# A routed-expert kernel whose token list gets rows of 16 equal words

## The chip, the cores and the metric

The kernel runs on one core of one Trainium2 chip. The metric is device time in microseconds of one execution, inputs and outputs in device memory. Five engines work side by side, each on its own instruction stream: TensorE (PE, with its weight loads PEld), VectorE (DVE), ScalarE (ACT), GpSimd (POOL) and SyncE (SP), which only issues transfers here. Transfers go through 16 DMA engines that all queues share; SP's plain transfers are queue q1 of the profile, POOL's indexed transfers are queue q0.

## The reference

```
# attention: a key counts for a query only if both fall to the same centroid
q_assign = argmax(q_n @ c_n, -1);  k_assign = argmax(k_n @ c_n, -1)
attn_out = softmax(where(q_assign == k_assign, q @ k.T / 8, -1e9)) @ v   # batch 2, 8 heads, 768 x 64
x = attn_out as (1536 tokens, 512)
# routed experts: one of 8 for each token
logits = x @ w_gate + modality_bias[modality_id];  e_idx = argmax(logits, 1)
for e in range(8):
    mask = e_idx == e
    out[mask] = gate_w[mask, None] * (relu(x[mask] @ w1[e]) @ w2[e])     # 512 -> 1024 -> 512
# a dense layer with softplus: 512 -> 2048 -> 512
return softplus(out @ w_in) @ w_out
```

## The kernel before, in words

**Attention.** The 16 pairs of batch and head are walked in 96 query tiles of 128 rows (6 a head). Tile g issues the score matmuls of tile g + 2, the transposes of tile g, and small jobs that a table hangs on g. The mask of a head pair is written into 16 partitions of the score operands `qB` and `kB` by four small SP transfers (`put_mask`, L295). After each head pair the attention rows go to `x_rows` in device memory (L394): each of 768 rows gets a run of 128 fp32 words, 512 bytes.

**Routing.** The tokens are routed in two batches of 768. `route_rank` gives each token a row number in `token_list`, a table in device memory: expert e owns rows from 1536 e on, with further rows for a late unit. The tokens of one expert stand one behind the other in their order. `scatter_list` (L594) then writes the token's number to that row: six indexed transfers on POOL, one for each 128 tokens, from column t of the tile `tokid`, through the helper `scatter` (L586), which also sets a spacer between two of them (L588, L589). The list starts out filled with the number 65536, which stands for "no token": `init_list` (a job of tile 7) sets up constants on POOL, fills the tile `empty` and stores it with one SP transfer (L1035, L1036).

**Expert units.** The expert stage is a written-out sequence of steps. A unit is a slice of one expert's list, of 256, 128 or 32 tokens. `u_list` (L754) reads the unit's token numbers with an SP transfer into the tile `it`, one word to a partition and column; `u_gather` (L768) clamps them on POOL into `gi` (L772) and fetches the 2 KB token rows with indexed transfers into `xg` (L776); `u_xpose` transposes `xg` on TensorE (L785); two layers follow (`l1_part` L818, `l2_part` L843), and the result rows go to `y_rows` with indexed transfers, 2 KB a row, again through `scatter`. Units 0 and 1 take tokens of the first batch alone; all later ones wait for the second batch's list. In the sequence, the transposes of unit 2 stand on TensorE ahead of the second layer of unit 1.

**Queues.** SP issues in program order, and so does POOL. On SP the first list read after the second `scatter_list` stands between weight loads (L730, L736): the loads written behind it are issued after it. Each weight chunk of 512 KB is split into two parts by ACT and by DVE or POOL (L740, L741) before TensorE uses it.

**The end.** When all units are written, `y_rows` is read back, and the dense layer runs over six blocks of 256 tokens (L1489, L1524).

Of the kernel before, what the change touches and what calls it, by code (L numbers as in the profile page):

```python
# [12 lines left out]
U32 = mybir.dt.uint32  # L13
# [19 lines left out]
def body(ctx, tc, qT, kT, vP, cen, mod, wg, bias, w1, w2, win, wout, out):  # L33
    nc = tc.nc
# [4 lines left out]
    NT = S // 128  # L39
# [2 lines left out]
    DUMMY = E * CAP  # L42
    LATE = DUMMY + 256 * NF
    LROWS = LATE + 256
    NM = N // 256
    CW = 1024
    pe, dve, act, pool, sp = nc.tensor, nc.vector, nc.scalar, nc.gpsimd, nc.sync

    xd = nc.dram_tensor("x_rows", (N, DM), F32, kind="Internal").ap()
    yd = nc.dram_tensor("y_rows", (N, DM), F32, kind="Internal").ap()  # L50
    lst = nc.dram_tensor("token_list", (LROWS, 1), U32, kind="Internal").ap()
    wf = nc.dram_tensor("w_rows", (16, 128, 1024), F32, kind="Internal").ap()

    const = ctx.enter_context(tc.tile_pool(name="const", bufs=1))
# [10 lines left out]
    def ctile(shape, dt, name):  # L65
        return const.tile(shape, dt, name=name)
# [2 lines left out]
    desc8 = ctile([128, E], F32, "desc8")  # L69
    tri = ctile([128, 128], BF16, "tri")  # L70
    ones = ctile([128, 128], BF16, "ones")
    tokid = ctile([128, 2 * NT], U32, "tokid")
    gate = ctile([128, 2 * NT], F32, "gate")
    lbias = ctile([128, 2 * NT, E], F32, "lbias")
    lacc = [ctile([128, NT, E], F32, f"lacc{b}") for b in range(2)]
# [29 lines left out]
    def setup_late():  # L105
        pool.iota(desc8, pattern=[[-1, E]], base=E, channel_multiplier=0, allow_small_or_imprecise_dtypes=True)
        pool.iota(e_off, pattern=[[CAP, E]], base=0, channel_multiplier=0, allow_small_or_imprecise_dtypes=True)
        pool.iota(tokid, pattern=[[128, 2 * NT]], base=0, channel_multiplier=1)
        pool.memset(e_row, 0.0)
        pool.iota(e_row[0:1], pattern=[[0, NT + 1], [CAP, E]], base=0, channel_multiplier=0, allow_small_or_imprecise_dtypes=True)  # L110
        pool.memset(e_row[0:1, NT, :], 0.0)
        pool.iota(iota_u, pattern=[[1, 16]], base=0, channel_multiplier=0, allow_small_or_imprecise_dtypes=True)
        pool.iota(u_fix, pattern=[[0, 3], [1, NK]], base=0, channel_multiplier=0, allow_small_or_imprecise_dtypes=True)
        for i, b in enumerate((128, 32, 0)):
            pool.iota(thr[:, i, :], pattern=[[256, 6]], base=b, channel_multiplier=0, allow_small_or_imprecise_dtypes=True)
        dve.tensor_reduce(out=fold, in_=ident.rearrange("p (g t) -> p t g", g=4), axis=AX.X, op=ALU.add)
        pool.iota(x_row, pattern=[[CAP, 9]], base=0, channel_multiplier=0, allow_small_or_imprecise_dtypes=True)
        pool.memset(ones, 1.0)
        pool.memset(tri, 1.0)
        pool.affine_select(  # L120
            out=tri, in_=tri, pattern=[[1, 128]], base=0, channel_multiplier=-1,
            compare_op=ALU.is_gt, fill=0.0,
        )
        pool.memset(pre9, 1.0)
        pool.affine_select(
            out=pre9, in_=pre9, pattern=[[1, 9], [-1, E]], base=0, channel_multiplier=0,
            compare_op=ALU.is_gt, fill=0.0,
        )
        pool.memset(drow, 0.0)
        pool.memset(nunit, 0.0)  # L130
        pool.memset(d_row, 0.0)
# [11 lines left out]
    p_1 = at.enter_context(tc.tile_pool(name="m1", bufs=1))  # L143
# [442 lines left out]
    def scatter(kind, **kw):  # L586

        pool.memset(spacer, 0.0)  # L588
        ins = pool.indirect_dma_start(**kw)  # L589
        for o in scattered[kind] + (scattered["y"] if kind == "late" else []):  # L590
            tc.declare_no_dep(ins.ins, o.ins, reason="rows are all different")
        scattered[kind].append(ins)

    def scatter_list(b, idx):  # L594
        for t in range(NT):
            scatter(
                "list", out=lst, out_offset=bass.IndirectOffsetOnAxis(ap=idx[:, t:t + 1], axis=0),
                in_=tokid[:, b * NT + t:b * NT + t + 1], in_offset=None,
            )

    def pick_early(cnt):
# [152 lines left out]
    def u_list(u, eng=sp):  # L754
        b = u["base"]
        if not isinstance(b, int):
            b = eng.value_load(b, min_val=0, max_val=DUMMY + 256 * (NF - 1))
        it = small.tile([128, 2], U32, tag="it", name="it", bufs=NF + NHU + NTU + 3)
        gi = small.tile([128, 2], U32, tag="gi", name="gi", bufs=NF + NHU + NTU + 3)
        with nc.allow_non_contiguous_dma(reason="token lists are columns of words"):  # L760
            if u["tiny"]:
                eng.dma_start(out=it[:32, 0:1], in_=lst[bass.ds(b, 32)])
            else:
                n = u["n"]
                eng.dma_start(out=it[:, :n], in_=lst[bass.ds(b, 128 * n)].rearrange("(j p) o -> p (j o)", p=128))
        u["it"], u["gi"] = it, gi

    def u_gather(u):  # L768
# [175 lines left out]
    with tc.manual_schedule():  # L944
# [57 lines left out]
        for p in range(1, 8):  # L1002
            b = 12 * (p - 1)
# [24 lines left out]
                    busy.add(g0 + k)  # L1028
            after.setdefault(g0 + 4, []).append((cv_store, (j,)))

        e_t = p_1.tile([128, LROWS // 128], U32, name="empty")

        def init_list():
            setup_late()
            pool.memset(e_t, int(EMPTY))  # L1035
            sp.dma_start(out=lst.rearrange("(p c) o -> p (c o)", p=128), in_=e_t)  # L1036
# [14 lines left out]
        def r0_scatter():  # L1051
            scatter_list(0, tmp["idx"])
            for i, u in enumerate((U0, U1)):
                u["eap"] = early[0:1, 2 * i:2 * i + 1]
                u["base"] = early[0:1, 2 * i + 1:2 * i + 2]
# [4 lines left out]
        job(65, route_carry)  # L1060
        job(80, route_gate, 0)
        job(81, lambda: u_list(U0))
        job(82, lambda: u_list(U1))
        job(84, lambda: u_gather(U0))
        ch0 = {}
# [26 lines left out]
        for g in range(NH * NT):  # L1092
            h, t = divmod(g, NT)
# [66 lines left out]
        for i in range(NEARLY, LF + 1):  # L1160
            t = i - NEARLY
# [144 lines left out]
        for k in loads[1]:  # L1306
            load(k)
        splits(1)
        scatter_list(1, idx)
        for f in range(4):  # L1310
            l1_part(U0, 1, f)
# [20 lines left out]
        def y_T(u, j):  # L1332
            if u >= NM:
                return
            i = 2 * u + j
            if j == 0:
                pl = xtp if u % 2 == 0 else xtp2
                yT[u] = tuple(pl.tile([128, 4, 256], F32R, tag=n, name=n) for n in ("xh", "xl"))
            to_T(yts.pop(i), *yT[u], j, bank=ps_A.tile([128, 512], F32, tag="a", name="bank") if j else None)
            y_load(i + 3)  # L1340
# [73 lines left out]
        for n in range(2, end):  # L1414
            kind, i, layer, s = seq[n]
# [96 lines left out]
        def m_l2(u, s, js=(0, 1)):  # L1512
            if u not in ys:
                ys[u] = [ps_T.tile([128, 512], F32, tag="t", name="o") for _ in range(2)]
            gh, gl = gs[u, s]
            for f in range(4):
                kt = 4 * s + f
                hi, lo = wts["out", kt // 2]
                k = (kt % 2) * 512
                wh, wl = hi[:, k:k + 512], lo[:, k:k + 512]  # L1520
                for j in js:
                    a = f * 256 + j * 128
                    for i, (x, y) in enumerate(((gh, wh), (gh, wl), (gl, wh))):
                        pe.matmul(ys[u][j], x[:, a:a + 128], y, start=(kt == 0 and i == 0), stop=(kt == 15 and i == 2))  # L1524
            if s == 3:
                for j in js:
                    y = ys[u][j]
                    o = yp.tile([128, DM], F32, tag="ysb", name="osb")
                    if j == 0:
                        act.copy(o, y)  # L1530
                    else:
                        dve.tensor_copy(o, y)
                    r = u * 256 + j * 128
                    sp.dma_start(out=out[r:r + 128], in_=o)


        def split_left(eng, cp=act.copy):
            nonlocal kl
            split(left.pop(0), eng, cp)
            if kl < NC:  # L1540
                load(kl)
                kl += 1

        while left and left[0] < NC - 8:
            split_left(dve)
        for u in range(NM):
            for s in range(4):
# [13 lines left out]
        for s in range(4):  # L1561
            m_l2(NM - 1, s, [0])

        o = yp.tile([128, DM], F32, tag="ysb", name="osb")
        for c, y in enumerate((ys[NM - 1][1], ps_A.tile([128, 512], F32, tag="a", name="o"))):
            cs = slice(c * 256, c * 256 + 256)
            for kt in range(16):
                gh, gl = gs[NM - 1, kt // 4]
                hi, lo = wts["out", kt // 2]
# [51 lines left out]
```

## Time and profile before

| what | value |
|---|---|
| runs | 753.99, 756.45, 763.52 us; median 756.45 us |
| profiled execution | 757.96 us, of which 756.2 us from the first to the last instruction |
| TensorE (PE) busy | 706.8 us, 93% |
| VectorE (DVE) busy | 455.2 us, 60% |
| ScalarE (ACT) busy | 392.6 us, 52% |
| GpSimd (POOL) busy | 157.1 us, 21% |
| mean granted TensorE clock | 0.986 |
| read from device memory, written | 79.13 MB, 18.28 MB |

The busy share of TensorE is high, but it is a mean over stages. What a change in the routing is worth is read in the microseconds between the second batch's list and the first matmul that needs it, and in the stretches ahead and behind.

### The profile page before, as it was taken

To read this page: it belongs to the slowest core of one execution; us is meant where nothing else is said; L and a number is where in the kernel's file an instruction comes from. 1 tells how busy PE (TensorE), PEld (TensorE's weight loads), DVE (VectorE), ACT (ScalarE), POOL (GpSimd) and SP (SyncE) were. 2 spreads that over 40 slices of the span, in tenths; PEclk is the share of its full clock that TensorE was granted. 3 is DMA by queue.
4 is the path that set the end of the run, shared out by engine and by line. 5 is a ranking of instruction groups with operands and counts; after the bars stand their busy time and mean duration, and the time that the engine had idled before them with its cause. 6 is when DMAs were issued, how large, how long until landed. Compare 5 with 4: busy or idle time off the path is not lost. (4 is left out here: it accounts for less than half of the span.)

```text
span 756.2 us, 11743 instructions
## 1 busy us (share of the span) xinstructions
PE 706.8 (93%) x4498; PEld 565.8 (75%) x4498; DVE 455.2 (60%) x668; ACT 392.6 (52%) x635; POOL 157.1 (21%) x172
## 2 busy tenths in 40 slices
PE   4898999899899989968999999998999999999998
PEld 2665665665566656857888879998899899899887
DVE  5898997899799975934546554686323324223220
ACT  3777886888678865524556553643332322323310
POOL 4301210111411205624542430261000000000000
PEclk9999999999999999997999999999999999999999
DMA  4317355453645344879868974500010000000000
GB/s 135 105 28 269 118 172 186 159 173 117 203 114 210 122 164 150 184 183 384 317 211 293 394 276 154 181 1 29 1 43 15 29 15 29 1 1 29 1 29 28
DMA packets 38683, 99.29 MB, mean 131 GB/s; under 512 B 8254, under 2 KB 15614, under 8 KB 36576
## 3 DMA queue, kind: packets, MB, share of 16 engines
q1 hardware_dynamic: 35888, 91.42, 36.4%
q0 software_dynamic: 2592, 6.69, 2.5%
q8 instruction: 36, 0.59, 0.3%
q10 hardware_dynamic: 144, 0.39, 0.2%
q14 instruction: 23, 0.19, 0.1%
HBM read 79.13 MB, written 18.28 MB: 129 GB/s over the span
## 5 line engine op out<-in xcount | busy, mean ns | idle before, releaser
L1500 DVE SCALAR_TENSOR_TENSOR sp<-g,sp 128x1024 f32<-128x1024 f32 x24 | 29.4, 1224 | 148.8 <-ACT sp L1499 148.8
L1489 PE MATMUL g<-xh,wh 128*128 128x256 f32 x384 | 108.7, 283 | 0.0
L1489 PE MATMUL g<-xh,wl 128*128 128x256 f32 x384 | 107.9, 281 | 0.0
L1489 PE MATMUL g<-xl,wh 128*128 128x256 f32 x384 | 107.9, 281 | 0.0
L330 ACT ACTIVATE P<-S,nm 128x768 f32<-128x768 f32 x96 | 87.0, 907 | 37.0 <-DVE nm L321 34.5
L343 PE MATMUL Tp<-ident,P 128*128 128x128 f32 x576 | 85.5, 282 | 14.0 <-ACT PT L348 8.9
L321 DVE TENSOR_REDUCE nm<-S 128x1 f32<-128x768 f32 x96 | 90.7, 946 | 8.9 <-PE S L319 8.6
L1497 ACT ACTIVATE sp<-g 128x1024 f32<-128x1024 f32 x24 | 24.6, 1027 | 136.6 <-PE g L1489 126.7
L343 PEld LDWEIGHTS Tp<-ident,P 128*128 128x128 f32 x576 | 68.9, 144 | 27.0 <-ACT PT L348 14.5
L741 POOL TENSOR_TENSOR wl<-raw,wh 128x1024 fp32r<-128x1024 f32 x22 | 54.1, 2467 | 135.2 <-ACT wh L740 128.2
L355 PE MATMUL av<-PT,v 128*64 128x384 f32 x384 | 79.8, 511 | 0.0
L741 DVE TENSOR_TENSOR wl<-raw,wh 128x1024 fp32r<-128x1024 f32 x50 | 65.2, 1344 | 14.7 <-ACT wh L740 14.7
L740 ACT CAST wh<-raw 128x1024 fp32r<-128x1024 f32 x69 | 68.9, 1050 | 9.6 <-DMA raw<-in_w 6.8
L1489 PEld LDWEIGHTS g<-xl,wh 128*128 128x128 f32 x384 | 73.0, 190 | 0.5
L1489 PEld LDWEIGHTS g<-xh,wh 128*128 128x128 f32 x384 | 72.8, 190 | 0.5
L1489 PEld LDWEIGHTS g<-xh,wl 128*128 128x128 f32 x384 | 73.0, 190 | 0.0
L348 ACT COPY PT<-Tp 128x384 f32<-128x384 f32 x144 | 64.1, 483 | 16.4 <-PE Tp L343 15.7
L1524 PE MATMUL o<-wh,gT 128*128 128x512 f32 x216 | 69.8, 394 | 0.0
L304 PEld LDWEIGHTS S<-kA,qA 128*128 128x128 f32 x192 | 30.1, 197 | 50.2 <-issue 14.5
L304 PE MATMUL S<-kA,qA 128*128 128x384 f32 x192 | 61.1, 401 | 3.8 <-ACT P L330 3.5
L843 PE MATMUL y<-wh,hT 128*128 128x512 f32 x192 | 64.5, 407 | 0.0
L818 PE MATMUL h<-xh,wh 128*128 128x256 f32 x192 | 55.1, 287 | 0.5 <-DVEq L1346 0.5
(284 smaller groups left out, 1402.3 us busy)
## 6 DMA issues: line engine op xcount, KB each, us to landing
raw<-in_w SPq DMA_DIRECT2D x56, 512.0 KB, 7.4
words<-in_win SPq DMA_DIRECT2D x8, 1024.0 KB, 7.0
w_rows<-cvt SPq DMA_DIRECT2D x16, 512.0 KB, 3.0
words<-in_wout SPq DMA_DIRECT2D x8, 1024.0 KB, 7.5
whole<-in_w SPq DMA_DIRECT2D x16, 512.0 KB, 5.6
raw<-w_rows SPq DMA_DIRECT2D x16, 512.0 KB, 5.4
rawq<-in_qT SPq DMA_DIRECT2D x8, 384.0 KB, 3.3
v<-in_vP SPq DMA_DIRECT2D x8, 384.0 KB, 5.2
```

The lines of the kernel that those rows point to most:

```text
L304: pe.matmul(ps[:, i, :HS], qA[:, t * 128:t * 128 + 128], kA[:, i * HS:(i + 1) * HS], start=True, stop=False)
L321: dve.tensor_reduce(out=nm_t[g], in_=ps[:, :, :HS], axis=AX.XY, op=ALU.max, negate=True)
L330: act.activation(out=P_t[g], in_=S_t.pop(g)[:, :, :HS], func=AF.Exp, bias=nm_t.pop(g), scale=1.0, accum_out=sums[h][:, t:t + 1],)
L343: pe.transpose(ps[:, j, :], P[:, i, j * 128:(j + 1) * 128], ident)
L348: act.copy(dst, ps)
L355: pe.matmul(av_t[h][64 * a:64 * a + 64, :], vt[p][:, kt, 64 * i:64 * i + 64], PT[h][:, kt, a * HS:(a + 1) * HS], start=(kt == 0), stop=(kt ...
L740: cp(self.hi, self.raw)
L741: eng.tensor_tensor(out=self.lo, in0=self.raw, in1=self.hi.bitcast(F32), op=ALU.subtract)
L818: pe.matmul(o, a, b[:, kt, :], start=(n == 0 and f % 2 == 0), stop=(n == 11), skip_group_check=True)
L843: pe.matmul(u["y"][j], x, y, start=(kt == 0 and i == 0), stop=(kt == 7 and i == 2))
L1489: pe.matmul(o, a, b[:, kt, :], start=(n == 0 and f % 2 == 0), stop=(n == 11), skip_group_check=True)
L1524: pe.matmul(ys[u][j], x[:, a:a + 128], y, start=(kt == 0 and i == 0), stop=(kt == 15 and i == 2))
```

## The change

The list's rows grow from one word to 16 equal words (`LW`). The tile of token numbers gets 16 copies of each number, the scatter writes a whole row of 64 bytes, the reads take the first word of each row, and the tile that fills the list at the start grows with it, from 104 to 1664 words a partition. The number of rows, of instructions and of transfers stays.

```diff
+    LW = 16
...
-    lst = nc.dram_tensor("token_list", (LROWS, 1), U32, kind="Internal").ap()
+    lst = nc.dram_tensor("token_list", (LROWS, LW), U32, kind="Internal").ap()
...
-    tokid = ctile([128, 2 * NT], U32, "tokid")
+    tokid = ctile([128, 2 * NT, LW], U32, "tokid")
...
-        pool.iota(tokid, pattern=[[128, 2 * NT]], base=0, channel_multiplier=1)
+        pool.iota(tokid, pattern=[[128, 2 * NT], [0, LW]], base=0, channel_multiplier=1)
...
-                in_=tokid[:, b * NT + t:b * NT + t + 1], in_offset=None,
+                in_=tokid[:, b * NT + t, :], in_offset=None,
...
-                eng.dma_start(out=it[:32, 0:1], in_=lst[bass.ds(b, 32)])
+                eng.dma_start(out=it[:32, 0:1], in_=lst[bass.ds(b, 32), 0:1])
...
-                eng.dma_start(out=it[:, :n], in_=lst[bass.ds(b, 128 * n)].rearrange("(j p) o -> p (j o)", p=128))
+                eng.dma_start(out=it[:, :n], in_=lst[bass.ds(b, 128 * n), 0:1].rearrange("(j p) o -> p (j o)", p=128))
...
-        e_t = p_1.tile([128, LROWS // 128], U32, name="empty")
+        e_t = p_1.tile([128, LROWS // 128 * LW], U32, name="empty")
```

## Rows read from the trace of the kernel before

**Rows 1.** Waits of TensorE, whole span: us in total, times, longest.
```profile
PE misc L785 <- DMA xg<-x_rows,gi: 10.2, 1, 10.2
```

**Rows 2.** Stretches: us, busy by engine (instructions), granted clock, DMA share, GB/s.
```profile
333.00:343.00 10.00, 0.00 (x0) 0.01 (x1) 1.74 (x2) 0.99 (x1) 6.49 (x8) 0.74 0.73 264
343.00:348.00 5.00, 4.97 (x14) 4.13 (x15) 1.98 (x2) 3.42 (x4) 3.59 (x4) 0.50 0.90 305
350.00:400.00 50.00, 50.00 (x358) 42.62 (x356) 25.97 (x25) 25.88 (x33) 20.50 (x23) 1.00 0.83 290
```

**Rows 3.** Timeline of TensorE around the wait: start, us, what, [idle before].
```profile
332.59 0.28 PE L818 MATMUL h<-xh,wl 128*128 128x256 f32 x1
343.02 1.08 PE L785 MATMUL misc<-ident,xg 128*128 128x128 f32 x4 [10.15 <-DMA xg<-x_rows,gi]
```

**Rows 4.** Timeline of SP, 317 to 334 us, starts and durations of its issues.
```profile
317.57 0.87 SPq L736 DMA_DIRECT2D whole<-in_w  x2
333.02 0.38 SPq L765 DMA_DIRECT2D it<-token_list  x1
```

**Rows 5.** Waits of SP, 318.5 to 334 us.
```profile
SPq L765 <- DMA token_list<-tokid,ridx: 13.6, 2, 11.0
```

**Rows 6.** Timeline of POOL, 310 to 336 us: the second batch's scatters.
```profile
310.00 1.02 POOL L589 DMA_INDIRECT token_list<-tokid,ridx  x1 [0.89 <-DVE nn L673]
...
311.32 0.98 POOL L589 DMA_INDIRECT token_list<-tokid,ridx  x1 [0.21 <-issue]
...
315.16 4.34 POOL L589 DMA_INDIRECT token_list<-tokid,ridx  x1 [0.22 <-issue]
...
319.81 2.56 POOL L589 DMA_INDIRECT token_list<-tokid,ridx  x1 [0.21 <-issue]
335.15 0.21 POOL L772 TENSOR_SCALAR gi<-it 128x2 uint32<-128x2 uint32 x1 [12.78 <-DMA it<-token_list]
```

**Rows 7.** DMA issues, 320 to 324 us: the last scatter; count, us to landing.
```profile
token_list<-tokid,ridx POOLq DMA_INDIRECT x1, 13.0
```

**Rows 8.** DMA queues, 308 to 312 us: packets, MB, share of 16 engines.
```profile
q1 hardware_dynamic: 368, 1.31, 80.0%
```

**Rows 9.** DMA queues, 312 to 316 us.
```profile
q1 hardware_dynamic: 16, 0.07, 111.5%
q0 software_dynamic: 64, 0.00, 1.2%
```

**Rows 10.** DMA queues, 341 to 345 us, with two scatters of 2 KB rows.
```profile
q1 hardware_dynamic: 289, 1.06, 70.4%
```

**Rows 11.** DMA queues, 205 to 209 us, with the first batch's scatters.
```profile
q1 hardware_dynamic: 33, 0.11, 28.7%
```

**Rows 12.** Line 589 from 340 us on, scatters to y_rows: landing times.
```profile
DMA to landing us min/median/max: 3.7/6.0/7.7
```

**Rows 13.** Line 765, the list reads: landing times.
```profile
DMA to landing us min/median/max: 2.1/7.5/9.9
```

**Rows 14.** DMA issues, whole span: count, KB each, median us to landing.
```profile
words<-in_win SPq DMA_DIRECT2D x8, 1024.0 KB, 7.0
...
x_rows<-xb SPq DMA_DIRECT2D x8, 384.0 KB, 3.1
...
kB<-mk SPq DMA_DIRECT2D x30, 24.0 KB, 1.9
```

**Rows 15.** Timeline of POOL, 30 to 44 us: the fill, and the next work.
```profile
31.11 0.17 POOL L1035 MEMSET empty<- 128x104 uint32 x1
42.14 0.83 POOL L278 TENSOR_SCALAR kA<-rawk 64x768 fp32r<-64x768 f32 x1 [10.85 <-PE S L304]
```

**Rows 16.** Timeline of TensorE, 26 to 50 us.
```profile
44.25 0.52 PE L319 MATMUL S<-kB,qB 80*128 80x384 f32 x2
```

**Rows 17.** Waits of TensorE, 195 to 260 us, after the first scatters.
```profile
PE Tp L343 <- ACT PT L348: 3.0, 4, 2.1
...
PE Tp L343 <- DVE pm L613: 0.6, 1, 0.6
```

## The prediction

> **What bounds the kernel now.** I read TensorE's waits first, because its busy share leaves little else to gain. In the whole span one wait stands out: the transposes of the first unit that holds second-batch tokens wait 10.2 us, once, for gathered rows [rows 1]. The reader sees the hole in the timeline: the first layer of unit 1 ends at 332.87 (332.59 + 0.28), the transposes start at 343.02 [rows 3]. The table of stretches then shows two things: from 350 to 400 us TensorE is busy 50.00 of 50.00 us, so what is given back at the hole is not lost to another wait there; and the granted clock, 0.74 in the mean of the hole, is 0.50 from 343 to 348: five microseconds of matmuls at the lower level (1.2 instead of 2.4 GHz) after the engine had stood idle [rows 2].
>
> Next I followed the hole back. The gather waits for the list read, which SP issues at 333.02; SP's issue before it ended at 318.44 (317.57 + 0.87) [rows 4], and what SP waits for in between is the landing of the list scatters [rows 5]. So the chain is scatter, list read, clamp, gather, transpose, with nothing else on it. The scatters start at 310.00, the second at 311.32, the last only at 319.81, since the fifth takes 4.34 us where the second takes 0.98, and the last 2.56 [rows 6]. The last lands 13.0 us after its start [rows 7], at 332.8.
>
> Are these 13 us the scatter's own, or queueing? The DMA queues answer. From 308 to 312 us, 368 packets of the weight loads take 80.0% of 16 engines [rows 8]: 0.80 x 16 x 4 us / 368 = 139 ns each. From 312 to 316, with the scatters' words under way, 16 such packets take 111.5%: 1.115 x 64 / 16 = 4.46 us each, 32 times as long, while the 64 packets of the scatter itself take 12 ns each [rows 9]. So from the first scatters on nearly everything on the 16 engines stands still. It is not indexed writing as such: beside two scatters of 2 KB rows, load packets take 0.704 x 64 / 289 = 156 ns [rows 10]. Beside the first batch's word scatters they take 0.287 x 64 / 33 = 557 ns [rows 11]. The hold-up goes with writes of single words into device memory.
>
> **The change part by part.** *The scatter's rows.* Twelve instructions stay; each writes 128 rows of 64 bytes instead of 4. The trace has no such write, so I bound it. From above, no relief: 13.0 us to landing [rows 7]. From below, the fastest of the scatters with 2 KB rows, 3.7 us; their median is 6.0, their slowest 7.7 [rows 12]. A second neighbour is the store of attention rows in runs of 512 bytes, 384 KB in a median of 3.1 us [rows 14]: short runs as such need not hold up anything. In ratio, 64 bytes lie 16 times above the word and 8 times below that run; I take the nearer, healthy side, and 6.0 us. The rows also stop sharing 64 bytes: with 128 tokens over 8 experts some 16 neighbouring words, one 64-byte stretch, were written by one transfer; now each row has its own.
>
> The Trainium skill speaks against this change: its page "DMA: Bandwidth & Descriptors", section Specifications, gives 512 B as the least transfer for line rate and says that below it the engine does read-modify-write. No run here shows rows between 4 and 512 bytes; by that rule the 64-byte rows stay on the slow side and the sum would be zero, which is the second case below.
>
> *The sum on the path.* POOL's pace without the long issues is 1.32 us (311.32 - 310.00), so the last scatter starts at 310.00 + 5 x 1.3 = 316.5 instead of 319.8. I take the two long issues as part of the hold-up, since the others of that group take about 1 us. Landing at 316.5 + 6.0 = 322.5 (320.2 by the lower bound, 324.2 by the slowest 2 KB scatter, 329.5 with the present 13.0). SP is free from 318.44 on and issues the read 0.2 us later, at 322.7. From the read to the transposes it took 343.02 - 333.02 = 10.0 us; unchanged, they can start at 332.7, just when the first layer of unit 1 ends (332.87). The wait goes from 10.15 us to nothing, or to 1.5 us with the later landing. With so short a wait I take the clock to stay up, as it did for part of the present one (its mean there, 0.74, is above 0.50), and the 5 us at 0.50 become 2.5. Gain: 10.15 + 2.5 = **12.6 us**; with the later landing 11.1.
>
> *The reads.* Nine of them, with as many words, each now from its own 64 bytes. The one on the path took 335.15 - 333.02 = 2.1 us to its user [rows 4, 6]; SP waits there, so nothing is queued ahead of it. Bounds: 2.1 as now, and 7.5, the median where loads are queued [rows 13]. I take 2.1; the other end is a case below. The later reads precede their use by whole steps, whose cover is the unbroken work from 350 on [rows 2].
>
> *The start.* The fill grows 16-fold: from 0.17 us to at most 16 x 0.17 = 2.7 us; the number tile grows from 12 to 192 words, less than that. POOL's next work starts at 42.14, after 10.85 us without any [rows 15], so at most 5.4 us more are covered. SP's store behind the fill becomes 832 KB; the larger load of 1024 KB lands in 7.0 us [rows 14], so from the fill's present start it lands by 31.1 + 2.7 + 2.7 + 7.0 = 43.5 at the latest. Behind it in the queue stand the four mask copies of the third head, which land in 1.9 us now [rows 14]; that head's first matmul with the masked operands starts at 44.25 [rows 16]. Scaled from the fill's row alone the numbers tile costs far less than 2.7 us, so I count zero; where every bound is met at once, 43.5 + 1.9 - 44.25 = 1.2 us.
>
> *What is late next.* The weight loads behind the read on SP move forward by the same 10 us, so TensorE and its supply move together; the clock's 2.5 us must come out of slack, of which rows 2 show no lack. The first batch's scatters get lighter too, but TensorE's four waits after them, 5.2 us in all, are for ScalarE and VectorE [rows 17]; I count nothing.
>
> **The number.** The profiled execution took 757.96 us (span 756.2, 1.8 outside), 1.5 above the median of 756.45. Against itself: 757.96 - 12.6 = 745.4; against the median, 743.9. I take 744.5. Two per cent, 15.1 us, is about what a measurement of this kernel can tell from no change, so my own forecast lies within it.
>
> **The rivals.**
> *No relief* (chance 0.14): 64-byte rows hold up the engines like words. For it: the gap between 4 and 512 bytes is not shown. The time stays at 756.5 to 758.
> *Half* (0.09): the scatter lands early, but the read now meets loads that its own release or the restored flow put on the engines, 7.5 instead of 2.1 us: transposes at 338.1, wait 5.2, gain 5, perhaps a microsecond of clock: 751 to 752. Against it: SP holds everything back until the scatters have landed.
> *Worse* (0.05): the hold-up goes by separate 64-byte stretches touched, not by words. Six scatters touched some 8 x 6 = 48 of them, now 768. The place is the same, the landing of the last scatter; the price is the hold-up beyond a healthy landing, 332.8 - 322.5 = 10.3 us, times its growth. It decides as soon as the landing falls behind 332.8; at 2.5 times it costs 15.5 us, 773. Against it: nothing but the 2 KB and 512-byte rows, which touch more and hold up nothing [rows 10, 14].
> *More* (0.06): the first batch's hold-up also sat on the path, up to those 5.2 us: 739 to 741.
> *Forecast* (0.66): 741 to 748, with the spread of the runs; about a sixth of it falls below 741.3.
>
> **How the numbers follow.** Faster by over 2% (below 741.3): 0.06 + 0.11 = 0.17. Slower by over 2%: 0.05. Within: 0.78. The range must take in the forecast's spread, half a gain, and most of no relief: 740 to 757.
>
> **What would show it.** Right: scatters of about 1 us each on POOL, the last landing by 324; load packets near 140 ns from 312 to 316; SP's read near 322.7; no hole ahead of the transposes, and the clock at 1.00 behind them. Wrong: load packets of microseconds beside the scatters as before (no relief), a read of over 5 us (half), a wait by the third head's scores at 44 us (the start), or a new wait of TensorE for weights from 335 to 450 us.

## The result, and the profile after

The changed kernel takes 751.01 us (median of four runs, 742.52 to 752.67), the kernel before 757.98 us beside it (four runs, 753.99 to 763.52). The ratio is 0.9877 with a 95% interval of 0.9831 to 0.9923: 6 to 13 us less, a gain, but under two per cent. The forecast was 744.5 us, in a range of 740 to 757.

The profiled executions are 757.96 us before and 749.72 us after (span 748.0): 8.24 us less. TensorE's waits, whole span, answer to [rows 1]:

```profile
PE misc L786 <- DMA xg<-x_rows,gi: 2.9, 1, 2.9
```

The hole is still there, but 2.9 us long instead of 10.2. Its two edges in TensorE's timeline answer to [rows 3]:

```profile
333.24 0.28 PE L819 MATMUL h<-xh,wl 128*128 128x256 f32 x1
...
336.41 1.09 PE L786 MATMUL misc<-ident,xg 128*128 128x128 f32 x4 [2.89 <-DMA xg<-x_rows,gi]
```

The left edge stands 0.65 us later (333.52 against 332.87), the right edge came forward from 343.02 to 336.41. Stretches behind it, with the columns of [rows 2] (busy by PE, PEld, DVE, ACT and POOL, then the granted clock, DMA share, GB/s):

```profile
336.00:339.00 3.00, 2.59 (x8) 2.25 (x9) 0.69 (x1) 1.41 (x2) 2.60 (x5) 0.50 1.05 386
339.00:343.00 4.00, 4.00 (x18) 3.32 (x17) 2.90 (x2) 2.01 (x3) 2.42 (x2) 0.96 1.04 381
343.00:348.00 5.00, 5.00 (x25) 4.15 (x25) 3.57 (x4) 2.48 (x3) 0.00 (x0) 1.00 1.02 411
350.00:400.00 50.00, 50.00 (x376) 43.63 (x375) 25.07 (x24) 26.98 (x34) 23.16 (x24) 1.00 0.83 294
```

After the shorter wait the granted clock still fell to 0.50 (1.2 instead of 2.4 GHz), for 2.59 us of work instead of 5. The two terms of the prediction's sum come to: wait 10.15 - 2.89 = 7.26 us, clock 2.5 - (2.59 x 0.50 + 4 x 0.04) = 1.05 us, together 8.3. That this meets the pair's 8.24 so closely is in part luck. Up to the hole the kernel after is 0.65 us behind. From the transposes to the end it is some 1.6 us quicker (748.0 - 336.41 = 411.6 against 756.2 - 343.02 = 413.2), of which the clock explains 1.05; the rest is not placed. From 350 to 400 us TensorE is busy throughout in both kernels, so nothing was given back there.

Where the remaining 2.89 us come from is read one step back. POOL's timeline, which answers to [rows 6]:

```profile
310.61 1.06 POOL L590 DMA_INDIRECT token_list<-tokid,ridx  x1 [0.16 <-DVE nn L674]
...
311.98 0.98 POOL L590 DMA_INDIRECT token_list<-tokid,ridx  x1 [0.21 <-issue]
...
315.81 4.34 POOL L590 DMA_INDIRECT token_list<-tokid,ridx  x1 [0.21 <-issue]
...
320.45 2.56 POOL L590 DMA_INDIRECT token_list<-tokid,ridx  x1 [0.23 <-issue]
...
328.40 0.21 POOL L773 TENSOR_SCALAR gi<-it 128x2 uint32<-128x2 uint32 x1 [5.39 <-DMA it<-token_list]
```

The fifth and sixth issue take 4.34 and 2.56 us, to the hundredth as before. SP's timeline then shows the read at 326.56, answering to [rows 4]:

```profile
318.23 0.88 SPq L737 DMA_DIRECT2D whole<-in_w  x2
...
326.56 0.39 SPq L766 DMA_DIRECT2D it<-token_list  x1
```

And the DMA queues from 312 to 316 us (packets, MB, share of 16 engines), answering to [rows 9]:

```profile
q1 hardware_dynamic: 62, 0.21, 16.7%
q0 software_dynamic: 96, 0.02, 3.1%
```

A load packet beside the scatters takes 0.167 x 64 / 62 = 172 ns instead of 4.46 us. The hold-up on the queues is gone; the long issues on POOL are not. VectorE's timeline shows what runs beside them:

```profile
314.10 1.20 DVE L826 SCALAR_TENSOR_TENSOR hT<-h,hT 128x1024 fp32r<-128x1024 f32 x1
...
315.83 3.47 DVE L742 TENSOR_TENSOR wl<-raw,wh 128x1024 fp32r<-128x1024 f32 x3
...
319.83 2.34 DVE L742 TENSOR_TENSOR wl<-raw,wh 128x1024 fp32r<-128x1024 f32 x2
```

The fifth issue (315.81 to 320.15) lies over three of VectorE's weight splits, the sixth (320.45 to 323.01) over most of two more. Either ends some 0.85 us after the last of its passes (319.30 and 322.17). The pass of L826, whose source `h` is in PSUM, lies over 0.77 us of the fourth issue, which takes 0.97 us.

The sixth scatter then lands 5.9 us after its start, of which the issue is 2.56 (DMA issues, 320.3 to 320.6 us; count, us to landing):

```profile
token_list<-tokid,ridx POOLq DMA_INDIRECT x1, 5.9
```

### The profile page after: what moved, and what is told of

The parts are those of the page before. It is cut to its first block, busy times and chain, and to the rows that moved or that the text cites. A ratio compares the mean times of both kernels' runs of the same rounds, so it can differ in the third digit from the quotient of the medians.

```text
span 748.0 us, 11745 instructions
## 1 busy us (share of the span) xinstructions
PE 704.7 (94%) x4498; PEld 564.3 (75%) x4498; DVE 454.7 (61%) x668; ACT 391.8 (52%) x635; POOL 161.4 (22%) x172
## 5 line engine op out<-in xcount | busy, mean ns | idle before, releaser
L344 PEld LDWEIGHTS Tp<-ident,P 128*128 128x128 f32 x576 | 68.7, 144 | 27.5 <-ACT PT L349 14.7
L742 DVE TENSOR_TENSOR wl<-raw,wh 128x1024 fp32r<-128x1024 f32 x50 | 65.2, 1343 | 14.3 <-ACT wh L741 14.3
```

Source lines behind the costliest of these rows:

```text
L344: pe.transpose(ps[:, j, :], P[:, i, j * 128:(j + 1) * 128], ident)
L742: eng.tensor_tensor(out=self.lo, in0=self.raw, in1=self.hi.bitcast(F32), op=ALU.subtract)
```

## Experiments

Theory A is the prediction's: words of one scatter that share 64 bytes of device memory hold up the DMA engines, rows of 64 bytes don't. Its rival was that any short write does. For the long issues the rivals were room in the queue (the prediction's view), VectorE's passes over two operands in SBUF, and the kind of instruction of those passes. The ratios are to the kernel before, run in the same rounds; *first to read* is from the first scatter of the second batch to SP's list read in the trace (23.0 us before, 16.0 after), *wait* is the one in [rows 1]; (one) marks a single run.

| kernel | median us | ratio, 95% | first to read | wait |
|---|---|---|---|---|
| splits by another instruction, on after | 749.64 | 0.9906 [0.9876, 0.9937] | 14.7 | 1.8 |
| the same on before | 758.02 | 1.0011 [0.9979, 1.0043] | 23.0 | 10.0 |
| 64-byte rows, first word written | 749.31 (one) | | 15.4 | 2.5 |
| rows of 16 bytes | 750.79 (one) | | 15.6 | 3.0 |
| VectorE held, on after | 748.82 | 0.9855 [0.9819, 0.9890] | 12.0 | 2.8 |
| VectorE held, on before | 759.05 | 1.0002 [0.9977, 1.0027] | 20.5 | 10.2 |
| list read first, on after | 750.58 | 0.9881 [0.9838, 0.9925] | 11.9 | none for `xg` |
| held and list read first, on after | 744.41 | 0.9805 [0.9768, 0.9843] | 8.8 | none |
| the same on before | 751.48 | 0.9877 [0.9837, 0.9917] | 14.2 | 2.2 |
| after, again, beside the holds | 748.70 | 0.9857 [0.9815, 0.9899] | 14.5 | 2.1 |
| after, again, beside list first | 751.04 | 0.9900 [0.9865, 0.9935] | 14.3 | 2.1 |

**One word in a row of 64 bytes.** The list keeps its rows, but the scatter writes only the first word of each; the read takes that word.

```diff
-    out=lst, ... in_=tokid[:, b * NT + t, :]
+    out=lst.rearrange("r (w o) -> (r w) o", o=1), ... in_=tokid[:, b * NT + t, 0:1]     # indices times LW
```

> The changed kernel's list of 64-byte rows, but each scatter writes only the first word of a row (indices times 16); 4 bytes a token as before, 64 bytes apart as after. Theory A (the hold-up comes from words of one transfer that share 64 bytes): no hold-up, load packets near 150 ns, first four scatters land in 2 to 5 us, wait of about 3 us. Theory B (it comes from writes shorter than some size, wherever they lie): the hold-up is back, load packets of several us, landings of 6.5 to 13 us, wait near 10 us, time 756 to 760.

**Rows of 16 bytes.** `LW = 4` instead of 16, so four rows share 64 bytes.

> The changed kernel with rows of 4 words: 16 bytes a token, four tokens to 64 bytes. By theory A (sharing) the hold-up shrinks to about a quarter: landings of 3 to 6 us, load packets up to 1 or 2 us, wait 3 to 5 us. By theory B (short writes) it stays as with words: landings 6.5 to 13 us, wait near 10 us.

The DMA queues from 312 to 316 us, first of the kernel with one word in 64 bytes, then of the one with 16-byte rows:

```profile
q1 hardware_dynamic: 162, 0.55, 33.9%
q0 software_dynamic: 64, 0.00, 1.2%
```

```profile
q1 hardware_dynamic: 60, 0.20, 49.9%
```

That is 0.339 x 64 / 162 = 134 ns for a load packet beside writes of 4 bytes, and 0.499 x 64 / 60 = 532 ns beside rows of 16 bytes; before it was 4.46 us, with the same 4 bytes in each write. (In other windows of 4 us up to 320 us, the one-word kernel shows up to 251 ns.) So it is how close together the writes of a transfer lie, not how short they are. Rows of 16 bytes are in between in the queues (915 ns a packet from 313 to 317), but the single run's time doesn't show it; its wait is 3.0 us, about that of after, and the late issues on POOL, 4.34 and 2.56 us there too, can cover the difference. That the stretch not to be shared is 64 bytes is only bracketed: 16 bytes apart is too close, 64 is not, and 32 was not tried.

**The splits by another instruction**, on after and on before, in the step that lies beside the scatters.

```diff
-    eng.tensor_tensor(out=self.lo, in0=self.raw, in1=self.hi.bitcast(F32), op=ALU.subtract)
+    if stt:
+        dve.scalar_tensor_tensor(
+            out=self.lo, in0=self.raw, scalar=1.0, in1=self.hi.bitcast(F32), op0=ALU.mult, op1=ALU.subtract
+        )
+    else:
+        eng.tensor_tensor(out=self.lo, in0=self.raw, in1=self.hi.bitcast(F32), op=ALU.subtract)
...
+    if n == 2:
+        split(k, dve, act.copy, True)
+        continue
```

> The changed kernel, with the five weight splits that VectorE makes while the second list is scattered written as scalar_tensor_tensor (raw x 1.0 - hi) instead of tensor_tensor; same numbers, same places. My theory: the scatter's two long issues on GpSimd (4.34 and 2.56 us) last because VectorE's 128x1024 tensor_tensor runs beside them; they fall to about 1.0 us, the last scatter starts near 317 and lands by 320, the list read is issued by 320.5 instead of 326.6, the wait of 2.9 us ahead of the transposes is gone, the clock stays at 1.00, and the time falls by 4 to 5 us against the changed kernel (about 745). First rival: the fifth and sixth indexed transfers in a row wait for room in their own queue; the issues stay at 4.34 and 2.56 us, and the time stays at 749 to 752. Second rival: any VectorE pass over two operands of this size does it, whatever the instruction; also unchanged.

> The kernel before (rows of one word), with the same five splits as scalar_tensor_tensor. My theory: the long issues go to about 1.0 us here too, but the hold-up by single words stays: load packets of several us beside the scatters, and the last scatter, started near 316.5, lands 7 to 13 us later, at 323 to 330 instead of 332.8; the wait of 10.2 us falls to 0.5 to 7, the time to 749 to 755. Rival (the long issues come from the queue that the words hold up): issues unchanged, wait near 10, time as before, 756 to 760.

Of the five splits that the expectation speaks of only the first three, those of that step, became the other instruction. On after, POOL's and VectorE's timelines:

```profile
312.78 4.35 POOL L590 DMA_INDIRECT token_list<-tokid,ridx  x1 [0.23 <-issue]
...
317.43 2.56 POOL L590 DMA_INDIRECT token_list<-tokid,ridx  x1 [0.22 <-issue]
```

```profile
312.80 3.48 DVE L743 SCALAR_TENSOR_TENSOR wl<-raw,wh 128x1024 fp32r<-128x1024 f32 x3
...
316.81 2.34 DVE L747 TENSOR_TENSOR wl<-raw,wh 128x1024 fp32r<-128x1024 f32 x2
```

The issue beside the three takes 4.35 us as with the old instruction, and the times don't move (on before, ratio 1.0011). So the kind of instruction is not the cause. What these three share with the old ones, and L826 does not, is that both operands are in SBUF.

**VectorE held** until POOL has issued the six scatters, on after and on before, by a copy of one word into a new 1x1 tile `hold`.

```diff
     scatter_list(1, idx)
+    pool.memset(spacer, 0.0)
...
+    if n == 2:
+        dve.tensor_copy(hold, spacer)
     splits(n)
```

> The changed kernel, with VectorE held before its five splits until GpSimd has issued the last list scatter (a one-word copy that waits for one more spacer). The splits themselves are tensor_tensor as in the changed kernel, some 2 to 3 us later. My theory after the first experiments: whatever the instruction, VectorE's 128x1024 passes over two SBUF operands stretch the indexed transfers that GpSimd issues beside them. The fifth and sixth issue fall from 4.34 and 2.56 to about 1.0 us, the six end 7.7 us after the first starts, the last lands within 2 to 4 us, the list read is issued some 6 us earlier than in the changed kernel, the wait of 2.9 us ahead of the transposes is gone and the clock stays at 1.00 there: 745 to 747, 3 to 5 us under the changed kernel. Rival: the fifth and sixth in a row wait for room in their queue; 4.34 and 2.56 us stay, and since VectorE is held longer still, the time is 751 to 756.

> The kernel before (rows of one word) with the same hold of VectorE. My theory: issues of about 1.0 us, but the hold-up by words stays, load packets of several us, landings of 7 to 13 us after the last start near 316.5: read at 324 to 330, wait of 1 to 7 us instead of 10.2, time 750 to 756. If the hold-up is set by the number of words alone and not by when they are issued, the words still drain until about 329 to 333 and the wait is 7 to 10 us, time as before.

POOL's, VectorE's and SP's timelines on after, and SP's wait:

```profile
318.15 0.97 POOL L591 DMA_INDIRECT token_list<-tokid,ridx  x1 [0.22 <-issue]
...
319.43 0.97 POOL L591 DMA_INDIRECT token_list<-tokid,ridx  x1 [0.22 <-issue]
```

```profile
320.51 0.14 DVE L1462 COPY hold<-spacer 1x1 f32<-1x1 f32 x1 [2.27 <-POOL spacer L1312]
```

```profile
316.52 5.75 SPq L732 DMA_DIRECT2D raw<-in_w  x2
...
323.11 0.88 SPq L738 DMA_DIRECT2D whole<-in_w  x2
...
325.01 0.39 SPq L767 DMA_DIRECT2D it<-token_list  x1
```

```profile
SPq L732 <- DVE wl L743: 4.9, 1, 4.9
```

All six issues take about 1 us, and the last lands at 321.54, 2.1 us after its start. A fifth and sixth issue in a row can be as short as the others, so the queue-room theory falls, unless loads beside them take the room: the hold keeps back loads as well. The pair with the list read first, below, settles that. Yet the wait stays at 2.8 us. The loads that stand ahead of the list read on SP need a buffer that the held splits free, so SP waits 4.9 us and reads only at 325.01, 3.5 us after the list has landed; and the read then takes 6.5 us beside those loads, where it took about 2. On before the issues become 0.97 us as well, but the six scatters land 6.8 to 16.0 us after their starts, and the wait stays 10.2 us. So on before the long issues were covered by the landing; on after they are what is left.

**The list read first**: the read of the step goes ahead of the step's weight loads on SP. Alone on after, then with the hold on after, then with the hold on before.

```diff
-    for k in loads[n]:
-        load(k)
     if n == 2:
         for v in range(2):
             u_list(us.pop(0))
+    for k in loads[n]:
+        load(k)
```

> The changed kernel with SP's first two list reads moved ahead of the loads of their step (two raw chunks and one pair stored whole); VectorE as in the changed kernel, so the fifth and sixth issue stay at 4.34 and 2.56 us. My theory: with fewer loads beside it the last scatter, which starts 9.8 us after the first, lands 3 to 4 us later instead of 4.5 to 6; the read is issued 13 to 14 us after the first scatter instead of 14.5 to 16, the wait ahead of the transposes falls from 2 to 3 us to 0 to 1.5; time 2 to 4 us under the changed kernel if the moved loads have slack, else a new wait of TensorE for weights between 320 and 360 us. Rival (the read is bound by the scatter's issues alone): wait and time unchanged.

> The hold of VectorE and the reads ahead of the loads together. In the held version the scatters were all landed 8.5 us after the first started, but SP issued the read only 12.0 us after it, because loads ahead of it in program order waited for raw buffers that the held splits free. My theory: with that order turned, the read is issued within 9 us of the first scatter, lands in about 2 us since no load is beside it, and the transposes have their rows before TensorE asks: wait 0, clock 1.00 behind it, 4 to 5 us under the changed kernel, 743 to 746. Rival: the loads, now behind the read and behind the held splits, come too late: a wait of TensorE for weights between 320 and 360 us takes back the gain, 747 to 752.

> The kernel before, with rows of one word, and both edits of the best version so far: VectorE held until the scatters are issued, and the list reads ahead of the loads. It asks whether the wider rows are still needed then. My theory: words that share 64 bytes hold up the DMA engines on their own, with or without loads beside them; the last scatter, started 6.5 us after the first, lands 8 to 14 us later, the wait ahead of the transposes stays at 3 to 10 us, the time at 752 to 758. Rival (the words are slow only because loads are queued with them): landings of 2 to 4 us as with wide rows, no wait, 744 to 747.

Alone, the read goes out 11.9 us after the first scatter and the wait for `xg` is gone, but the loads now stand behind SP's wait for the landing, and two other waits of TensorE take its place:

```profile
PE misc L786 <- DVE xl L791: 1.6, 1, 1.6
...
PE th L881 <- ACT xh L789: 1.6, 1, 1.6
```

Both stand behind ScalarE, which from 318 to 356 us waits 11.7 us for `raw` chunks (3.1 in after). The time is that of after, and not the 2 to 4 us less that I expected. Nor did the issues stay at 4.34 and 2.56 us. POOL's fourth to sixth issue, and VectorE's splits beside them:

```profile
314.57 0.97 POOL L590 DMA_INDIRECT token_list<-tokid,ridx  x1 [0.21 <-issue]
...
315.84 3.41 POOL L590 DMA_INDIRECT token_list<-tokid,ridx  x1 [0.23 <-issue]
...
319.56 1.43 POOL L590 DMA_INDIRECT token_list<-tokid,ridx  x1 [0.23 <-issue]
```

```profile
314.94 3.47 DVE L742 TENSOR_TENSOR wl<-raw,wh 128x1024 fp32r<-128x1024 f32 x3
...
318.94 2.34 DVE L742 TENSOR_TENSOR wl<-raw,wh 128x1024 fp32r<-128x1024 f32 x2
```

The fifth is shorter because it begins 0.90 us into its three splits; it again ends 0.84 us after the last of them. The sixth begins 0.62 us into its two, as in after, but ends 0.85 us after the first of them (320.14), and not after the second; what let it through earlier is open. The fourth, which began 0.37 us ahead of a split, is not stretched. So a split beside an issue need not lengthen it by its whole time.

With both edits on after, POOL's and SP's timelines, and the stretches over the old hole:

```profile
318.16 0.97 POOL L591 DMA_INDIRECT token_list<-tokid,ridx  x1 [0.23 <-issue]
...
322.23 0.77 POOL L774 TENSOR_SCALAR gi<-it 128x2 uint32<-128x2 uint32 x1 [3.01 <-DMA it<-token_list]
```

```profile
320.49 0.39 SPq L767 DMA_DIRECT2D it<-token_list  x1
...
322.88 0.94 SPq L732 DMA_DIRECT2D raw<-in_w  x2
```

```profile
333.00:343.00 10.00, 10.00 (x58) 8.64 (x57) 7.55 (x15) 7.26 (x10) 3.14 (x2) 1.00 1.03 399
343.00:353.00 10.00, 10.00 (x70) 9.02 (x68) 3.06 (x3) 2.66 (x5) 2.15 (x1) 1.00 1.03 403
```

In this kernel and in the one with the list read first alone, SP issues no load from 306 us until the read; all that differs there is the hold of VectorE. The fifth and sixth issue take 3.41 and 1.43 us without it and 0.97 and 0.97 with it. So the long issues come from VectorE's splits, and not from loads or room in the queue.

No hole and no clock loss: TensorE is busy 10.00 of 10.00 us at a clock of 1.00. This is the best version, 744.41 us (742.41 to 746.79), 6.6 us under after in the same rounds, the intervals of the two ratios apart. Against before it is 12 to 18 us, and the 12.6 of the prediction's sum lies in that interval. Of the 6.6 us the two traces show 2.1, the wait; the two profiled executions lie only 0.5 us apart (746.78, among the slowest of its six, and 747.23, the fastest of its seven). Where the rest is stays open.

On before, with single words and both edits, DMA issues of the last scatter (microseconds from issue to landing), and the queues from 316 to 320 us, where no row of load packets is left:

```profile
token_list<-tokid,ridx POOLq DMA_INDIRECT x1, 7.5
```

```profile
q0 software_dynamic: 64, 0.00, 1.2%
```

Even with no loads beside them the words take 7.5 us to land, against 2.1 us for the last rows of 64 bytes in the held kernel. That is a little less than expected for them (8 to 14), and the wait is 2.2 instead of at least 3: part of the 13 us of [rows 7] was the words, part was the words together with the loads. Rows of 64 bytes seem worth 5 to 7 us there: 7.1 by the medians (751.48 against 744.41), 5.5 by the two ratios. The rounds are different ones, and the intervals of the ratios, 0.9837 to 0.9917 and 0.9768 to 0.9843, overlap a little.

**After, unaltered**, twice, as a control in the rounds of the holds and of the list reads.

> The changed kernel itself, unaltered, on the same chip and in the same rounds as the held version, for the difference between the two: 750 to 752 by all theories.

> The changed kernel itself once more, beside the two versions with the reads first, for the difference: 748 to 752 by all theories, wait of 2 to 3 us.

The controls give 748.70 (750 to 752 expected) and 751.04 us, so differences of 2 us between kernels of different rounds say nothing. Their waits are 2.1 us in both traces, and behind them the clock stays at 1.00; in after, with a wait of 2.89, it fell to 0.50. But the length of the wait alone does not decide it. The stretch around the wait of 2.8 us in after with VectorE held, then the one behind the wait of 2.2 us in before with both edits:

```profile
333.00:352.00 19.00, 16.15 (x93) 13.66 (x92) 13.27 (x20) 10.03 (x13) 12.15 (x11) 1.00 1.03 395
```

```profile
336.00:340.00 4.00, 4.00 (x14) 3.24 (x13) 2.09 (x3) 1.53 (x2) 3.10 (x4) 0.68 1.03 373
```

Over the traces of these kernels the clock stayed at 1.00 behind waits of 1.8, 2.1, 2.1, 2.5 and 2.8 us, and fell behind 2.2, 2.9, 3.0 and all of about 10.

## Why the prediction was right, and where its size was off

Of the 12.6 us forecast, 8.3 came: 2.89 us of the wait stayed, and 1.45 of the clock's 2.5.

**The mechanism** was right: the single words held the engines up, and rows of 64 bytes do not. The one-word experiment shows it with the read, the fill and the rows' places kept. The prediction drew from the page "DMA: Bandwidth & Descriptors" of the Trainium skill, section Specifications, that by its line of 512 B the change would do nothing, and gave that case a chance of 0.14. It did not come: load packets took 172 ns beside rows of 64 bytes, and 134 to 251 ns beside 4 bytes in 64. What rate the short writes themselves reached, no run here shows.

**The landing.** I took 6.0 us between 3.7 and 13.0. Undisturbed it is below my lower bound: the first four scatters of after land in 2.1 to 3.5 us, the six of the held kernel in 2.1 to 3.2. My neighbour, rows of 2 KB, moves 32 times the bytes. On the path of after the last scatter did land 5.9 us after its start, so the term came out; but 2.56 of that are the long issue, and that the two made up the 6.0 is luck.

**The issues: the step that failed.** I wrote "I take the two long issues as part of the hold-up", and let the last scatter start 6.5 us after the first. It starts 9.84 us after it, since the two issues stay at 4.34 and 2.56 us: 3.3 us more, and the wait that is left is 2.89. The issues follow VectorE's splits: hold VectorE and they are 0.97 us, in kernels of either row size, with the loads beside them or without. The other scatters of that group, which I gave as my reason, had no such split beside them; a look at VectorE's timeline over the same microseconds would have shown it. The page "SBUF — State Buffer" of the Trainium skill, section "SBUF: two separate sides", says that VectorE and GpSimd share a pair of ports as an exclusive lock, and that GpSimd can't write its descriptors while VectorE holds it. The runs agree with that effect (0.97 against 4.34 us); that it is this lock, they don't show. The page puts passes with two SBUF operands under the lock only against a GpSimd operation that reads SBUF; which kind an issue is, no run here shows.

**The clock.** I let it stay up behind a short wait and counted 2.5 us. With 2.89 us of wait it fell for 2.59 us of work, so 1.05 came. With no wait, which was the forecast, it stays at 1.00, as the best version shows. That it stays up behind any short wait does not hold: it stayed behind 2.8 us in one kernel and fell behind 2.2 in another, and what decides is open.

**The reads** went as counted: from SP's read to the transposes 336.41 - 326.56 = 9.85 us, forecast 10.0. That loads ahead of the read can make it 6.5 us (the rival "half") showed only in the held kernel.

**The start** was covered. The fill takes 1.48 us, between the bounds 0.17 and 2.7, and POOL still idles 9.09 us before its next work:

```profile
32.10 1.48 POOL L1036 MEMSET empty<- 128x1664 uint32 x1
...
42.66 0.83 POOL L279 TENSOR_SCALAR kA<-rawk 64x768 fp32r<-64x768 f32 x1 [9.09 <-PE S L305]
```

The 832 KB store lands in 3.3 us, and no wait of TensorE for the third head's masks appears.

**The rivals.** The measured median, 751.01 us, lies outside the 741 to 748 of the forecast's own case, which had a chance of 0.66. It lies at the lower end of "half" (751 to 752), but not by its mechanism: the read on the path was quick, 2 us to its user; the scatters were late. It fell into the stated range since that was wide enough for half a gain. Of the signs that I named for being right, the load packets came (172 ns, forecast 140); the last two issues, the last landing (326.4, forecast 324), SP's read (326.56, forecast 322.7), the hole and the clock behind it did not. "More" and "worse" did not occur: TensorE's waits from 195 to 260 us, after the first batch's scatters, are 5.2 us before (seven waits; the prediction says four) and 6.4 us after.

## What to carry to other kernels

When one small transfer stalls everything, ask which of its writes fall into the same stretch of device memory, and give each a stretch of its own before buying larger transfers. Split a late landing into start, issue and flight, and for each long issue look at every engine over the same microseconds before putting it down to the queue. A cause removed uncovers the next: here late issues, then the order on SP, and only both edits together brought the summed gain.

## What the runs showed of the hardware

Beside scatters of single words, load packets take 4.46 us; beside the same words 64 bytes apart 134 to 251 ns; beside rows of 16 bytes 532 to 915 ns. A POOL issue of an indexed write takes 0.97 us alone, 4.34 us (begun with the first of them) or 3.41 us (begun 0.90 us into it) beside three VectorE passes of 128x1024 with both operands in SBUF, each time until some 0.85 us after the last; it takes 0.97 us with a pass from PSUM beside 0.77 us of it. It seems to work the other way too: where the list is read first, one VectorE split, otherwise 1.2 us, took 3.20 us at 329.21 beside a split on POOL (328.90 to 331.32).
